# Attention backward on one core: row sums, transposes and casts of a softmax block moved by one to six units, and another order of the score products

## The chip, the cores and the metric

The kernel runs on one core of a Trainium2 chip. A core has a matrix engine (TensorE, PE in the profile, which keeps the loading of weights apart as PEld), three elementwise engines (VectorE or DVE, ScalarE or ACT, GpSimd or POOL), an engine that here only issues transfers (SyncE or SP), and 16 DMA engines. Each engine takes its own list of instructions in order and waits for the others through semaphores. The metric is the time of one execution on the device, in microseconds.

## The reference

Two attention blocks with 16 heads of width 28 over 2048 tokens of width 448 are evaluated forwards, their outputs are put side by side, and all gradients are returned (eight of them, and the output). Block A is linear attention. Block B, which fills most of the time, is softmax attention where all heads share one K and one V:

```python
q = (x @ wq).reshape(B, S, H, Dh)...        # 16 heads
k = x @ wk;  v = x @ wv                     # one for all heads
scores = einsum("bhqd,bkd->bhqk", q, k) * (Dh ** -0.5)
p = _softmax(scores, axis=-1)
o = einsum("bhqk,bkd->bhqd", p, v)
out = o... @ wo
...
_out, _vjp = jax.vjp(_f, A_x, ..., B_wo);  _grads = _vjp(grad_out)
```

Backwards, with do the gradient at o, the softmax needs dP = do v^T, dS = P * (dP - D) with D the row sums of do * o, then dQ = dS k, dK = dS^T q and dV = P^T do.

## The kernel before

Block A comes first, then the projections of block B, then the core of block B (the loop over `u`, L917), then the last products and gradients. The change touches only the core.

**Blocks and units.** The core works on 64 blocks `b`: 256 queries of two heads each. A block is cut into eight units of 256 keys, so there are 512 units, and unit `u` holds the scores of block u // 8. In unit `u` the scores S of that unit are made, together with dP (called D in the code, not to be mixed up with the row sums) of unit `w = u - 16`, two blocks earlier. Scores and dP are kept transposed: keys on the partitions, 512 columns for two times 128 keys, 256 queries each; one array for head 0 and one for head 1. Below, "position" is u mod 8, and S0, S1, D0, D1 are S and dP of heads 0 and 1. Each is two matmuls of 32 rows x 256 columns into one PSUM bank.

**What one unit does on each engine, in order.** The loop's body is the order, written out by hand (`tc.manual_schedule()`).

- TensorE: S and D (`rows_SD`, L663); in even units the products for o and dQ (`o_dq`) and dV (`dv_mm`), in odd units dK (`dk_m`, 16 matmuls at a time). Small products of other steps come in between: transposes of o (`onat_T`), transposes of do' (`don_T`), a part of an output projection.
- ScalarE: exp of S0 (L939), a copy `cp` of D1 (L953), exp of S1 (L997).
- VectorE: dsT of head 0, that is D0 times exp (L951), then the small steps that are due, then a 32x32 stream transpose `dsx` of a dsT made two units earlier (L1030).
- GpSimd: dsT of head 1, that is `cp` times exp (L956), and small steps, casts and copies.
- SyncE: every fourth unit a DMA transpose of the exponentials for dV (L999), in half of the blocks one of q for dK (L847), and five times in all one of o for the output projection (L988).

**Banks.** S has three PSUM banks in rotation: two are written in a unit and the third, `spare`, takes the small products (L921). After the units at positions 0, 2, 4 and 6 the spare bank is the one that S1 of the next unit writes; after positions 1, 3, 5 and 7 it is the one that S0 of the next unit writes. D has two banks, both written in each unit: D0's is free when VectorE's multiplication has read it, D1's when ScalarE's `cp` has.

**Steps that come once in a block.** `due(u, lag)` gives block `b` in unit 8b + lag. In order:

- lag 11 (position 3): o is scaled from its accumulator into `oTs` (VectorE, L972). The same accumulator holds dQ of block b - 2 in its other half, and a GpSimd cast (L978) stores that half as bf16 over q.
- lag 12 (position 4): `onat_T` transposes o into natural layout in the spare bank; `o_norm` takes the reciprocal of the softmax sums and makes `o_s` on VectorE, then on GpSimd `prod` = do * o (L812) and do' = `don` = do / sum (L815). The softmax sums are folded into do, and D into a column of do'.
- lag 13 (position 5): `row_D` sums `prod` over each head's columns (VectorE, L823), and GpSimd multiplies the result into the first column of `don` (L824).
- lag 14 (position 6): `don_T` transposes do' (L832, four matmuls into the spare bank); `don_copy` copies it as `doT` (VectorE, L839); `o_keep` casts `o_s` over do (GpSimd, L819), and for five blocks SyncE starts a DMA transpose of that.
- lag 16 (position 0 of the next block): the D products of block b begin, and read `doT`. The output projection's parts and their stores (L734) stand at position 0 too.

**The order of S and D.** `rows_SD` has a list `todo` of pairs (0 for S or 1 for D, head); each pair's first mention is its first 256 columns, its second mention the others. S of a head and D of a head lie in four different groups of 32 rows of the array.

Of the kernel before, what the change touches and what calls it, by code (L numbers as in the profile page):

```python
# [25 lines left out]
def kernel(  # L26
# [21 lines left out]
    nc = tc.nc  # L48
# [578 lines left out]
    NB = 64  # L627
    NU = NB * 8
    qT_B = [R1[:, g, :] for g in range(4)]
    vaug, kn, do_nat = vaug_, kn_, R2x[:, 0:NS, :]  # L630
    with ExitStack() as cs_:
# [17 lines left out]
        def eT(u):  # L649
            return ETs[u // 4 % 5][:, u % 4, :, :]  # L650
# [4 lines left out]
        def mmt(out, lhsT, rhs, pos, start, stop):  # L655
            nc.tensor.matmul(out, lhsT=lhsT, rhs=rhs, start=start, stop=stop, tile_position=pos,  # L656
                             skip_group_check=True)

        def blk(b):
            qc, pair = divmod(b, 8)  # L660
            return qc, pair, pair // 2, pair % 2

        def rows_SD(u, sp, dp):  # L663
            b, tp = divmod(u, 8)
            w = u - 16
            qc, pair, g, hp = blk(b)
            todo = [(0, 0), (0, 1), (1, 0), (1, 1)] * 2
            if sp is not None and dp is not None:
                todo = [(0, 0), (1, 0)] * 2 + [(0, 1), (1, 1)] * 2 if u % 2 else \
                    [(0, 0), (0, 1), (1, 0)] * 2 + [(1, 1)] * 2  # L670
            seen = {}
            for d in todo:
                if (dp if d[0] else sp) is None:
                    continue
                k, h = d
                t2 = seen.get(d, 0)
                seen[d] = 1
                t = 2 * tp + t2
                tc_ = slice(t * P, (t + 1) * P)
                oc = slice(t2 * 256, (t2 + 1) * 256)  # L680
                r = 64 * (1 - hp if k else hp) + 32 * h
                if k:
                    mmt(dp[h][:, oc], vT_rep[r:r + 32, tc_], doT[w // 8][r:r + 32, :], (r, 0), True, True)
                else:
                    mmt(sp[h][:, oc], kT_rep[r:r + 32, tc_], qT_B[g][r:r + 32, qc * 256:(qc + 1) * 256],
                        (r, 0), True, True)
# [7 lines left out]
        oTs = pp_.tile([P, 256], F32, name="oTs", bufs=1)  # L694
# [95 lines left out]
        def due(u, lag):  # L790
            b, r = divmod(u - lag, 8)
            return b if r == 0 and 0 <= b < NB else None

        def onat_T(b, bank):
            onp = bank[:, 0:P].rearrange("p (q h c) -> p q h c", q=2, h=2)
            r = 64 * (1 - b % 2)
            for qb in range(2):
                nc.tensor.transpose(onp[:, qb, :, :].rearrange("p h c -> p (h c)"), oTs[r:r + 64, qb * P:(qb + 1) * P],
                                    identF[r:r + 64, :], tile_position=(r, 0))
            onps[b] = onp  # L800

        def o_norm(b):
            onp = onps.pop(b)
            qc, pair, g, hp = blk(b)
            r_ = pw_.tile([P, 2, 2, 1], F32, name="rl")
            os_ = o_s[:]
            nc.vector.reciprocal(out=r_[:], in_=onp[:, :, :, 0:1])
            nc.vector.tensor_tensor(out=os_, in0=onp[:, :, :, :], in1=r_[:].to_broadcast([P, 2, 2, 32]), op=ALU.mult)  # L808
            rl[b] = r_
            dnv = do_nat[:, 2 * qc:2 * qc + 2, pair * 64:pair * 64 + 64].rearrange("p q (h c) -> p q h c", c=32)  # L810
            prod[b] = pw_.tile([P, 2, 2, 32], F32, name="prod", bufs=1)
            nc.gpsimd.tensor_tensor(out=prod[b][:], in0=dnv, in1=os_, op=ALU.mult)  # L812
            dn = pw_.tile([P, 2, 2, 32], BF16, name="don", bufs=2)
            don[b] = dn
            nc.gpsimd.tensor_tensor(out=dn[:], in0=dnv, in1=r_[:].to_broadcast([P, 2, 2, 32]), op=ALU.mult)  # L815
            o_nat[b] = dnv, os_

        def o_keep(b):
            nc.gpsimd.tensor_copy(out=o_nat[b][0], in_=o_nat.pop(b)[1])  # L819

        def row_D(b):
            Dq = pw_.tile([P, 2, 2, 1], F32, name="Dq")
            nc.vector.tensor_reduce(out=Dq[:, :, :, 0], in_=prod[b][:], axis=AX.X, op=ALU.add)  # L823
            nc.gpsimd.tensor_tensor(out=don[b][:, :, :, 0:1], in0=Dq[:], in1=rl[b][:], op=ALU.mult)  # L824

        def don_T(b, bank):
            r = 64 * (1 - b % 2)
            tp2 = bank[:, 0:P].bitcast(BF16)
            for qb in range(2):
                for h in range(2):  # L830
                    q = r + 32 * h
                    nc.tensor.transpose(tp2[q:q + 32, qb * P:(qb + 1) * P], don[b][:, qb, h, :], identB[:, :],  # L832
                                        tile_position=(0, q))
            tps2[b] = tp2

        def don_copy(b):
            r = 64 * (1 - b % 2)
            doT[b] = pw_.tile([P, 256], BF16, name="doT", bufs=2)
            nc.vector.tensor_copy(out=doT[b][r:r + 64, :], in_=tps2.pop(b)[r:r + 64, 0:256])  # L839
# [68 lines left out]
        with tc.manual_schedule():  # L908
# [8 lines left out]
            for u in range(NU + 28):  # L917
                w = u - 16
                hasS = u < NU
                hasD = 0 <= w < NU  # L920
                b0, b1, spare = ((SB[i] for i in ((0, 1, 2), (0, 2, 1), (1, 0, 2), (1, 2, 0))[u % 4]) if hasS else SB)  # L921
                sp = [b0, b1] if hasS else None
                dp = DB if hasD else None
                rows_SD(u, sp, dp)
                if u % 2 == 0:
                    o_dq((u - 4,), (u - 20,))
                if (b := due(u, 12)) is not None:
                    onat_T(b, spare)
                if (b := due(u, 14)) is not None:
                    don_T(b, spare)  # L930
                if op := out_part(u):
                    out_proj(*op, spare)
# [14 lines left out]
                if hasD:  # L947
                    dst = pd_.tile([P, 2, 512], BF16, name="dsT")
                    dsT[w] = dst
                    ew = eT(w)  # L950
                    nc.vector.tensor_tensor(out=dst[:, 0, :], in0=dp[0][:, :], in1=ew[:, 0, :], op=ALU.mult)  # L951
                    cp = pc_.tile([P, 512], BF16, name="cp")
                    nc.scalar.activation(out=cp[:, :], in_=dp[1][:, :], func=ACT.Copy)  # L953
                    if (b := due(u, 13)) is not None:
                        row_D(b)
                    nc.gpsimd.tensor_tensor(out=dst[:, 1, :], in0=cp[:, :], in1=ew[:, 1, :], op=ALU.mult)  # L956
                if (b := due(u, 13)) is not None and not hasD:
                    row_D(b)
                gq, iq = divmod(u % 64 - 30, 8)
                qq = u // 64 + 1  # L960
# [7 lines left out]
                if u % 8 == 3 and 0 <= (b := (u - 11) // 8) < NB + 2:  # L968
                    r = 64 * (1 - b % 2)
                    rr = slice(r, r + 64) if b < 2 else slice(0, P)  # L970
                    if b < NB:
                        nc.vector.tensor_scalar(out=oTs[rr, :], in0=oq[rr, 0:256], scalar1=fac[rr, b % 2:b % 2 + 1],  # L972
                                                scalar2=None, op0=ALU.mult)
                    if b >= 2:
                        qc, pair, g, hp = blk(b - 2)
                        rq = slice(64 * hp, 64 * hp + 64)
                        if b < NB:
                            nc.gpsimd.tensor_copy(out=qT_B[g][rq, qc * 256:(qc + 1) * 256], in_=oTs[rq, :])  # L978
                        else:
                            nc.vector.tensor_scalar(out=qT_B[g][rq, qc * 256:(qc + 1) * 256], in0=oq[rq, 0:256],  # L980
                                                    scalar1=scale, scalar2=None, op0=ALU.mult)
                if (b := due(u, 12)) is not None:
                    o_norm(b)
                if (b := due(u, 14)) is not None:
                    o_keep(b)
                    if b in (15, 31, 47, 55, 63):
                        t0, t1 = 2 * (b // 8) - 2 * (b < 48), 2 * (b // 8) + 2
                        nc.sync.dma_start_transpose(oTq[:, 4 * (t0 % 4):4 * (t0 % 4) + 4 * (t1 - t0), :],  # L988
                                                    do_nat[:, t0:t1, :].rearrange("p q c -> p (q c)"))
                if (b := due(u, 14)) is not None:  # L990
                    don_copy(b)
                if op:
                    out_store(*op, spare)
# [10 lines left out]
                if u % 2:  # L1004
                    b, i = divmod(u - 27, 8)
# [20 lines left out]
                if 0 <= y < NU:  # L1026
                    b, tp = divmod(y, 8)
                    if tp == 0:
                        dsx[b] = px_.tile([P, 8, 2, 2, 256], BF16, name="dsx")
                    nc.vector.transpose(  # L1030
                        out=dsx[b][:, tp, :, :, :].rearrange("p h t c -> p (h t c)").bitcast(F32),
                        in_=dsT[y][:, :, :].rearrange("p h c -> p (h c)").bitcast(F32))
# [113 lines left out]
```

## Time and profile before

The median of three runs is 1082.68 us (1082.59 to 1083.07).

| | us |
|---|---|
| profiled execution | 1082.19 |
| its span | 1080.1 |
| TensorE busy | 1050.2 |
| VectorE busy | 881.6 |
| ScalarE busy | 879.2 |
| GpSimd busy | 800.9 |
| TensorE's clock | full in all of the 40 slices |

The core runs from about 213 us, where the first exp starts, to about 1030 us. Of 300 to 998 us, 698 us, the engines are busy for 685.9 (TensorE), 683.6 (ScalarE), 653.0 (VectorE) and 635.7 (GpSimd). An entry of the timeline is: start, duration, engine, line, operation, output <- inputs, shapes, how many, and in brackets the idle time before it and who ended it. A line of the waits is: who waited, at which line, for whom: total, times, longest. Matmuls in the timeline overlap: several in different row or column groups of the array run at once. PSUM tiles go by the name of their pool: `aacc` is a bank of S (or the spare one), `agen` one of D, o, dQ or dK.

### The profile page before, as it was taken

The page shows a single profiled execution, that of the slowest core. Times are in us where ns is not written, and L with a number is a line of the kernel's source. Part 1 is how long each engine was busy: PE and PEld are TensorE (multiplying, and loading weights), DVE is VectorE, ACT ScalarE, POOL GpSimd, SP SyncE. Part 2 cuts the span into 40 slices and gives each one's busy share as a digit, 9 for nine tenths or more (in the row PEclk, how much of TensorE's full clock was granted, in tenths as well). Part 3 has the DMA queues.
Part 4 walks back from the last instruction along what each step waited for, and adds up shares of the span by engine and source line. Part 5 has one row for each costly group of instructions (what it writes and reads, how often), then busy time and mean ns, then how long its engine had stood idle before and what let it go on. Part 6 is the DMA issues. An engine that isn't in the chain of part 4 may idle for free.

```text
span 1080.1 us, 39972 instructions
## 1 busy us (share of the span) xinstructions
PE 1050.2 (97%) x16232; PEld 467.8 (43%) x16241; DVE 881.6 (82%) x1735; ACT 879.2 (81%) x1741; POOL 800.9 (74%) x1098
## 2 busy tenths in 40 slices
PE   9999999989999999999999999999999999999998
PEld 4555545433444444444444444444444444444434
DVE  7887400559999999999999999999999999999943
ACT  6463122589999999999999999999999999999622
POOL 6001252228998998899889989988998899888881
PEclk9999999999999999999999999999999999999999
DMA  9759898079999999999999999999999999999973
GB/s 269 157 109 195 178 203 230 13 142 195 197 193 191 175 191 186 190 190 202 176 183 186 193 197 184 194 191 175 194 189 188 191 196 194 178 180 177 213 149 92
DMA packets 689936, 195.14 MB, mean 181 GB/s; under 512 B 670616, under 2 KB 687792, under 8 KB 689752
## 3 DMA queue, kind: packets, MB, share of 16 engines
q1 hardware_dynamic: 680152, 179.92, 97.8%
q0 software_dynamic: 4640, 8.71, 2.6%
q10 hardware_dynamic: 4960, 3.96, 1.4%
q8 instruction: 127, 2.08, 0.8%
q14 instruction: 57, 0.47, 0.1%
HBM read 12.60 MB, written 10.84 MB: 22 GB/s over the span
## 4 chain that ended last, share of the span: by engine, by line
PE 43%; POOL 27%; ACT 15%; issue 8%; DVE 7%; POOLq 0%; ACTq 0%; DVEq 0%
POOL dsT L956 20%; PE agen L81 14%; PE agen L656 13%; ACT cp L953 8%; PE aacc L656 7%; PE aacc L81 7%; ACT eT L997 5%; DVE dsx L1030 3%; ACT eT L939 2%; POOL prod L812 2%; POOL R L978 1%; DVE dsT L951 1%; POOL don L815 1%; POOL qst L843 1%; PE aacc L832 1%
## 5 line engine op out<-in xcount | busy, mean ns | idle before, releaser
L956 POOL TENSOR_TENSOR dsT<-cp,eT 128x512 bf16<-128x512 bf16 x512 | 587.8, 1157 | 69.9 <-ACT cp L953 62.1
L1030 DVE STREAM_TRANSPOSE dsx<-dsT 128x512 f32<-128x512 f32 x512 | 357.5, 698 | 2.1 <-POOL dsT L956 0.9
L951 DVE TENSOR_TENSOR dsT<-agen,eT 128x512 bf16<-128x512 f32 x512 | 341.0, 666 | 20.7 <-PE agen L656 17.1
L656 PEld LDWEIGHTS <-R 128*32 128x32 bf16 (+1 forms) x9104 | 212.2, 93 | 313.2 <-issue 270.4
L939 ACT ACTIVATE eT<-aacc 128x512 bf16<-128x512 f32 x512 | 320.4, 626 | 20.8 <-PE aacc L656 17.3
L953 ACT ACTIVATE cp<-agen 128x512 bf16<-128x512 f32 x512 | 320.9, 627 | 12.9 <-PE agen L656 11.9
L997 ACT ACTIVATE eT<-aacc 128x512 bf16<-128x512 f32 x512 | 326.6, 638 | 0.0
L656 PE MATMUL agen<-doT,R 32*128 32x256 bf16 x2048 | 279.9, 269 | 2.9 <-DVE dsT L951 2.1
L656 PE MATMUL aacc<-R,R 32*128 32x256 bf16 (+1 forms) x2240 | 268.7, 268 | 3.6 <-ACT eT L939 1.8
L656 PE MATMUL agen<-dsx,qX 32*32 32x512 bf16 x4096 | 267.6, 375 | 0.0
L656 PE MATMUL agen<-dsT,R 128*32 128x256 bf16 x2048 | 188.4, 276 | 0.5 <-issue 0.5
L656 PE MATMUL agen<-eT,R 128*32 128x256 bf16 x2048 | 188.3, 276 | 0.1
L656 PEld LDWEIGHTS <-qX 32*32 32x32 bf16 x4096 | 79.8, 89 | 114.7 <-issue 54.3
L656 PE MATMUL aacc<-eN,don 128*32 128x512 bf16 x1024 | 96.7, 379 | 0.0
L81 PEld LDWEIGHTS <-R 128*128 128x128 bf16 (+1 forms) x517 | 40.7, 98 | 43.2 <-issue 11.0
L406 POOL COPY pk<-R 128x256 bf16<-128x256 bf16 x4 | 1.6, 397 | 73.8 <-DVE R L366 73.7
L81 PE MATMUL agen<-R,R 128*128 128x448 bf16 (+1 forms) x174 | 41.1, 360 | 1.3 <-issue 0.6
L823 DVE TENSOR_REDUCE Dq<-prod 128x4 f32<-128x128 f32 x64 | 18.3, 286 | 26.1 <-POOL prod L812 26.1
L812 POOL TENSOR_TENSOR prod<-R,o_s 128x128 f32<-128x128 bf16 x64 | 27.6, 432 | 11.2 <-DVE o_s L808 11.2
L843 POOL COPY qst<-R 128x512 bf16<-128x512 bf16 x56 | 34.3, 613 | 1.3 <-DMA qX<-qst 1.3
L656 PEld LDWEIGHTS <-don 128*32 128x32 bf16 x1024 | 33.8, 97 | 1.2 <-issue 0.7
L422 DVE TENSOR_TENSOR osb<-aacc,pr 64x448 bf16<-64x448 f32 x2 | 1.2, 617 | 38.8 <-DMA out_dram<-osb 24.2
(233 smaller groups left out, 975.7 us busy)
## 6 DMA issues: line engine op xcount, KB each, us to landing
out_dram<-osb ACTq DMA_DIRECT2D x22, 112.0 KB
eN<-eT SPq DMA_TRANSPOSE x128
xa<-in_A_x_dram SPq DMA_DIRECT2D x8, 224.0 KB
ga<-in_grad_out_dram SPq DMA_DIRECT2D x4, 448.0 KB
xa<-in_grad_out_dram POOLq DMA_DIRECT2D x4, 448.0 KB, 5.8
out_dram<-wdq POOLq DMA_DIRECT2D x8, 224.0 KB, 4.1
eT<-in_grad_out_dram SPq DMA_DIRECT2D x4, 448.0 KB
eT<-in_B_x_dram SPq DMA_DIRECT2D x4, 448.0 KB
```

The lines of the kernel that those rows point to most:

```text
L81: nc.tensor.matmul(out_ap, lhsT=lhsT, rhs=rhs, start=start, stop=stop, tile_position=(0, 0))
L656: nc.tensor.matmul(out, lhsT=lhsT, rhs=rhs, start=start, stop=stop, tile_position=pos, skip_group_check=True)
L812: nc.gpsimd.tensor_tensor(out=prod[b][:], in0=dnv, in1=os_, op=ALU.mult)
L815: nc.gpsimd.tensor_tensor(out=dn[:], in0=dnv, in1=r_[:].to_broadcast([P, 2, 2, 32]), op=ALU.mult)
L823: nc.vector.tensor_reduce(out=Dq[:, :, :, 0], in_=prod[b][:], axis=AX.X, op=ALU.add)
L843: eng.tensor_copy(out=st.rearrange("p (b s) a j -> p b s a j", s=2)[:, :, s, :, :], in_=src.unsqueeze(2).to_broadcast([P, 4, 4, 32]))
L939: nc.scalar.activation(out=eT(u)[:, 0, :], in_=sp[0][:, :], func=ACT.Exp, scale=scale)
L951: nc.vector.tensor_tensor(out=dst[:, 0, :], in0=dp[0][:, :], in1=ew[:, 0, :], op=ALU.mult)
L953: nc.scalar.activation(out=cp[:, :], in_=dp[1][:, :], func=ACT.Copy)
L956: nc.gpsimd.tensor_tensor(out=dst[:, 1, :], in0=cp[:, :], in1=ew[:, 1, :], op=ALU.mult)
L997: nc.scalar.activation(out=eT(u)[:, 1, :], in_=sp[1][:, :], func=ACT.Exp, scale=scale)
L1030: nc.vector.transpose(out=dsx[b][:, tp, :, :, :].rearrange("p h t c -> p (h t c)").bitcast(F32), in_=dsT[y][:, :, :].rearrange("p h c -> p ...
```

## The change

Five edits, all in the core's loop.

1. `row_D` at lag 14 instead of 13 (position 6).
2. `don_T` and `don_copy` at lag 15 instead of 14 (position 7, an odd unit; `don_T` stands behind S and D and ahead of dK).
3. The cast of dQ's half of `oTs` on GpSimd at lag 17 (position 1 of the next block) instead of lag 11 (position 3); the last two blocks keep their cast on VectorE at position 3.
4. `o_keep`, and with it the five DMA transposes of o, at lag 16 instead of 14 (position 0 of the next block).
5. In units that have both S and D, the odd ones issue S0, D0, D1, S1 and then the same four again, where they issued S0, D0 twice and then S1, D1 twice. Even units keep S0, S1, D0 twice and then D1 twice.

```diff
             todo = [(0, 0), (0, 1), (1, 0), (1, 1)] * 2
             if sp is not None and dp is not None:
-                todo = [(0, 0), (1, 0)] * 2 + [(0, 1), (1, 1)] * 2 if u % 2 else \
-                    [(0, 0), (0, 1), (1, 0)] * 2 + [(1, 1)] * 2
+                todo = [(0, 0), (1, 0), (1, 1), (0, 1)] * 2 if u % 2 else [(0, 0), (0, 1), (1, 0)] * 2 + [(1, 1)] * 2
...
-                if (b := due(u, 14)) is not None:
+                if (b := due(u, 15)) is not None:
                     don_T(b, spare)
...
-                    if (b := due(u, 13)) is not None:
+                    if (b := due(u, 14)) is not None:
                         row_D(b)
                     nc.gpsimd.tensor_tensor(out=dst[:, 1, :], in0=cp[:, :], in1=ew[:, 1, :], op=ALU.mult)
-                if (b := due(u, 13)) is not None and not hasD:
+                if (b := due(u, 14)) is not None and not hasD:
                     row_D(b)
...
                     if b >= 2:
                         qc, pair, g, hp = blk(b - 2)
                         rq = slice(64 * hp, 64 * hp + 64)
-                        if b < NB:
-                            nc.gpsimd.tensor_copy(out=qT_B[g][rq, qc * 256:(qc + 1) * 256], in_=oTs[rq, :])
-                        else:
+                        if b >= NB:
                             nc.vector.tensor_scalar(out=qT_B[g][rq, qc * 256:(qc + 1) * 256], in0=oq[rq, 0:256],
                                                     scalar1=scale, scalar2=None, op0=ALU.mult)
+                if (b := due(u, 17)) is not None and b >= 2:
+                    qc, pair, g, hp = blk(b - 2)
+                    rq = slice(64 * hp, 64 * hp + 64)
+                    nc.gpsimd.tensor_copy(out=qT_B[g][rq, qc * 256:(qc + 1) * 256], in_=oTs[rq, :])
                 if (b := due(u, 12)) is not None:
                     o_norm(b)
-                if (b := due(u, 14)) is not None:
+                if (b := due(u, 16)) is not None:
                     o_keep(b)
...
-                if (b := due(u, 14)) is not None:
+                if (b := due(u, 15)) is not None:
                     don_copy(b)
```

## The prediction

> **What bounds the kernel now.** I read the page first, then the waits of the long middle stretch (300 to 998 us), then the timeline of one block of eight units, instruction by instruction.
>
> ```profile
> PE 1050.2 (97%) x16232; PEld 467.8 (43%) x16241; DVE 881.6 (82%) x1735; ACT 879.2 (81%) x1741; POOL 800.9 (74%) x1098
> ```
>
> All four compute engines are nearly full, and TensorE's 97% counts a matmul as busy while it merely stands in the pipeline, so shares settle nothing. The waits of 300 to 998 us do:
>
> ```profile
> POOL dsT L956 <- ACT cp L953: 50.6, 144, 0.9
> PEld L832 <- POOL don L824: 26.7, 56, 0.9
> DVE Dq L823 <- POOL prod L812: 23.1, 55, 0.6
> ...
> ACT eT L939 <- PE aacc L656: 11.6, 54, 0.3
> ```
>
> 56 blocks lie there. In nearly every one TensorE waits for the last column of do' (L824; 0.48 us each), and VectorE for the product whose rows it sums (0.42). One block, positions 2 to 7, then 0 and 1 (u mod 8), starts at 698.94 and ends at 711.21:
>
> ```profile
> 699.88 0.67 ACT L953 ACTIVATE cp<-agen 128x512 bf16<-128x512 f32 x1
> ...
> 700.42 0.28 PE L656 MATMUL aacc<-R,R 32*128 32x256 bf16 x1
> ...
> 700.54 0.32 PE L656 MATMUL agen<-doT,R 32*128 32x256 bf16 x2
> 700.61 0.28 PE L656 MATMUL aacc<-R,R 32*128 32x256 bf16 x1
> 700.71 0.27 PE L656 MATMUL agen<-doT,R 32*128 32x256 bf16 x1
> 700.85 0.69 ACT L939 ACTIVATE eT<-aacc 128x512 bf16<-128x512 f32 x1
> ...
> 700.91 1.04 PE L656 MATMUL agen<-dsx,qX 32*32 32x512 bf16 x16
> ...
> 703.57 1.15 POOL L956 TENSOR_TENSOR dsT<-cp,eT 128x512 bf16<-128x512 bf16 x1
> ...
> 704.68 0.43 POOL L812 TENSOR_TENSOR prod<-R,o_s 128x128 f32<-128x128 bf16 x1
> ...
> 705.15 0.29 DVE L823 TENSOR_REDUCE Dq<-prod 128x4 f32<-128x128 f32 x1 [0.30 <-POOL prod L812]
> ...
> 705.58 0.22 POOL L824 TENSOR_TENSOR don<-Dq,rl 128x4 bf16<-128x4 f32 x1
> ...
> 705.85 0.23 PE L832 MATMUL aacc<-identB,don 128*32 128x128 bf16 x2
> ...
> 705.98 0.65 DVE L951 TENSOR_TENSOR dsT<-agen,eT 128x512 bf16<-128x512 f32 x1
> ...
> 706.50 0.28 PE L656 MATMUL aacc<-R,R 32*128 32x256 bf16 x1
> 706.66 0.29 DVE L839 COPY doT<-aacc 64x256 bf16<-64x256 bf16 x1
> 706.68 0.26 PE L656 MATMUL agen<-doT,R 32*128 32x256 bf16 x1
> ...
> 707.01 0.26 PE L656 MATMUL aacc<-R,R 32*128 32x256 bf16 x1
> ...
> 707.33 1.05 PE L656 MATMUL agen<-dsx,qX 32*32 32x512 bf16 x16
> ```
>
> Three things to see. First, the chain at position 6: product on POOL (704.68), row sum (705.15), column (705.58), transposes (705.85). VectorE's multiplication slips with it to 705.98, so position 7's first D product waits until that is done (706.68), and its S1 until the doT copy has emptied the spare bank (707.01). Second, 700.54: two D products in 0.32 us, the second starting 0.05 after cp ended (699.88 + 0.67 = 700.55). It sits in D's second bank; that release holds up the end of S/D in every odd unit. Third, ScalarE's three operations per unit start 0.48 apart when nothing holds them: 1.43 a unit, 11.5 a block, its floor.
>
> TensorE's S/D start times (698.94, 700.42, 701.88, 703.52, 705.01, 706.50, 708.31, 709.56, 711.21) give unit lengths of 1.48, 1.46, 1.64, 1.49, 1.49, 1.81, 1.25, 1.65: 12.27 us.
>
> **The change part by part.** I carry this block forward by hand, zero at 698.94, with spacings read from it. Release to dependent instruction: 0.05. Last needed S start to exp: 0.31. S/D end to the next kind of product: 0.20 after its last start. dK to the next unit's S/D: 0.98. A freed ScalarE operation lasts 0.60.
>
> (1) Row sum one unit later (13 to 14). VectorE's 0.42 wait goes. In position 5 it now goes straight from multiplication to stream transpose, and position 6's multiplication starts at 6.5 instead of 7.04. The product has long been ready then. POOL's column operation (0.22) now stands behind position 5's dsT multiplication as well: dsT of position 4 at 4.6, spacing 1.12, product 0.38, don 0.37, dsT of position 5 1.13, so the column runs 7.60 to 7.82. VectorE's sum ends at 7.4, so POOL's queue sets it.
>
> (2) Transposes from position 6 to 7 (14 to 15). Position 6 loses the wait and four transposes. S/D of 6 starts at 6.07; D1 waits for cp (6.16) until 6.22, its second half at 6.33; products at 6.52; four rounds and dV take 0.77 as at position 4; position 7 starts at 7.29 (now 7.56): 0.27 earlier. There the transposes stand alone between 32-row S/D and dK. The rows: 0.20 into the other shape, 0.06 for the second pair, 0.16 out (o to S/D takes 0.21 with a 0.11 product, so 0.10 beyond the product, plus 0.055): 0.42, against 0.20 for S/D to dK directly. So 0.22 of added TensorE time. The column at 7.82 plus 0.05 is before the 7.96 at which transposes could start: no wait, with 0.1 to spare.
>
> The Trainium skill speaks against this part: TensorEngine Tiling (Array Packing), Key Properties, says that changing the tiling mode drains the TensorE. The trace agrees in direction (0.20 instead of 0.11 between starts); a full drain would be the 0.27 that one S product lasts, on two switches instead of 0.20 and 0.16, and by that the block would lose 0.07 + 0.11 = 0.18 and the whole gain 62 x 0.18 = 11 us of what is worked out below. I go by the rows.
>
> (3) doT's copy now follows in position 7, and the unit right behind it uses it, and its bank for S0. VectorE: multiplication at 8.0, copy behind it 8.6 to 8.9, S0 possible from 8.95. TensorE arrives at 9.16. Hidden behind dK, slack 0.2; if VectorE ran later than that, every microsecond would be paid.
>
> (4) Odd order S0, D0, D1, S1 twice. The products take four row groups either way; the quoted 700.61 line follows D1 there, not S0's round. What changes: D1's wait for cp now stands ahead of the second halves of S0 and D0. TensorE's end of S/D does not move (D1, plus 0.11), but exp and VectorE's multiplication start from D1's release plus 0.31. In position 3: D1 at 1.66, exp at 1.98 instead of 1.91. At 5 S1 (waiting for o_s) does the same: 5.08 instead of 5.01. Cost 0.07 to 0.09 per odd unit on ScalarE's chain. In the walk below it mostly disappears, because S/D of the next unit starts when dK ends and not when exp does; and a late start shortens cp from 0.68 to 0.60. I take nothing at 3 and 5, and let 7 and 1 come out of the walk.
>
> (5) dQ cast (0.39) from position 3 to 1 of the next block, o's cast (0.29) from 6 to 0. POOL's sum stays: 8 x 1.13 + 0.37 + 0.38 + 0.37 + 0.2 + 0.25 = 10.6, with two qst copies 11.7, in a 12.0 block. Both leave the stretch from 3 to 6 where the column is made and enter 0 and 1, where dsT waits for cp. The oTs rewrite (2.6) follows the cast (1.3 to 1.65) by a unit. Cost zero, cover: two units before VectorE needs dsT. Without the cover: 0.68. The five DMA transposes of o on SP move two units, behind position 7's eN transpose (5.4 us on SP): issue, wait and 2.9 us make 8.3 of the eight units (12 us) before their reader. Hidden; five late ones would cost a few us in all. SP itself: two eN transposes (10.9) and one qX (1.3) make 12.2 in half of the blocks and 10.9 in the others: its mean, 11.6, stays under 12.0.
>
> **The sum.** Positions 2 to 5: 6.07 as now. Position 6: exp 6.52, cp 7.00 to 7.60. Position 7: start 7.29, D1 at 7.65, second halves 7.65, last product 7.76, transposes 7.96 and 8.02, dK 8.18, end 9.16; exp 7.97, cp 8.45 to 9.05. Position 0: D1 is free, so S/D takes 0.38 and not 0.50; with 0.75 behind it as now, it ends at 10.29; exp 9.59, cp 10.07 to 10.67. Position 1: D1 waits for that cp until 10.72, last product 10.83, dK 11.03, end 12.01. So 12.01 against 12.27, 0.26 less. Position 7 gets longer (1.87), position 1 too (1.72): the wait for cp takes over what don_T's wait gave up. exp spacings give 12.35 as mean block from unit 26 to 506. About 62 blocks x 0.26 = 16 us. The profiled execution took 1082.19 (span 1080.1), 0.5 below the median: 1066 either way.
>
> **Rivals.**
> A. Slower: the new order of odd units. If ScalarE, not TensorE, paces positions 1, 3, 5 and 7, the later exp of (4) is paid four times on top of the walk: 0.07 to 0.09 each, 0.28 to 0.36 a block against the 0.26 gained. It decides from 0.065 an odd unit on; at 0.09 the block is 0.10 longer than now: 1084 to 1089. For it: ScalarE's starts stand 0.48 apart from position 2 to 4. Against it: over the whole block ScalarE has 12.27 - 11.5 = 0.8 us to spare.
> B. Nothing: only exp at position 7 counts, 8.06 now and 7.97 then, and the rest is lost to D1's waits: 0.03 or less a block, 1081 to 1083. For it: position 6's gain of 0.27 shrinks to 0.09 there. Against: dK's end moves by 0.21.
> C. Larger: VectorE's freed 0.42 and POOL's earlier dsT also shorten positions 3 to 5 and 1, down to 11.75: 1050. ScalarE's floor, 11.5, would be 1034; nothing in the trace reaches it for a whole block.
> D. Less: POOL late. With qst copies and the store's DMA (0.58) in one block the column slips 0.26, past the 0.1 to spare. If the transposes wait 0.15 in every block: 12.16, 1075.
>
> **How the numbers follow.** Forecast (about 1058 to 1072) 0.44, C 0.12, D 0.16, B 0.06, A 0.22. About 0.2% is what a measurement here can tell from no change. Faster: 0.44 + 0.12 + 0.16 = 0.72; same 0.06; slower 0.22. The range reaches from C's near half (1052) to most of A (1087); the forecast's own is 1058 to 1072.
>
> **What would show it.** L832's wait for L824 and L823's for L812 gone; block near 12.0; position 6 near 1.22, positions 7 and 1 near 1.87 and 1.72; exp of odd units later by some 0.08 against their S/D start. It is wrong if L832 still waits for L824 (POOL), if S0 of position 0 waits for L839 (VectorE), or if ScalarE's odd units lengthen without TensorE waiting.

## The result: 0.55% faster, a third of what was forecast

The changed kernel takes 1077.26 us (median of four runs, 1076.81 to 1078.0) against 1082.88 before: ratio 0.9945, 95% interval 0.9928 to 0.9962. It is faster, clear of noise, but by 5.6 us and not by 16, and 1077 lies outside the forecast's own range (1058 to 1072). The profiled execution took 1077.67 us (span 1075.9).

The waits of 300 to 998 us in the changed kernel (who waited, for whom: total us, times, longest) (line numbers differ by one or less from those of before, save dQ's cast, which has its own place now):

```profile
POOL dsT L955 <- ACT cp L952: 44.2, 114, 0.6
DVE dsT L950 <- PE agen L656: 21.3, 85, 0.3
PEld L831 <- POOL don L823: 12.1, 57, 0.3
PEld aacc L797 <- ACT eT L998: 12.1, 57, 0.2
ACT eT L938 <- PE agen L656: 12.0, 58, 0.4
```

VectorE's wait for the product is gone (23.1 us), as forecast. The row of don_T and POOL's column is not: 12.1 us are left of 26.7, in all 57 blocks. It counts the idle time ahead of don_T's weight load (PEld), and not that ahead of its products (PE). The timeline of one block shows what each of them waited for (positions 6 and 7; S/D of position 6 starts at 702.90):

```profile
704.34 0.65 ACT L998 ACTIVATE eT<-aacc 128x512 bf16<-128x512 f32 x1
704.46 0.21 POOL L823 TENSOR_TENSOR don<-Dq,rl 128x4 bf16<-128x4 f32 x1
704.55 0.28 PE L656 MATMUL aacc<-R,R 32*128 32x256 bf16 x2
...
704.67 0.27 PE L656 MATMUL aacc<-R,R 32*128 32x256 bf16 x1
704.87 0.28 PEld L831 LDWEIGHTS <-don 128*32 128x32 bf16 x4 [0.21 <-POOL don L823]
704.88 0.60 ACT L938 ACTIVATE eT<-aacc 128x512 bf16<-128x512 f32 x1
...
705.04 0.29 PE L831 MATMUL aacc<-identB,don 128*32 128x128 bf16 x4
705.26 1.04 PE L656 MATMUL agen<-dsx,qX 32*32 32x512 bf16 x16
```

The column is ready at 704.46 + 0.21 = 704.67. The last S/D product starts at 704.67, so by my spacing of 0.20 the transposes were possible at 704.87, and that is when their weights are loaded. The products start at 705.04, which is 0.05 after the second exp of position 6 has ended (704.34 + 0.65 = 704.99). That exp empties the bank that S1 had in position 6, and that bank is the spare one of position 7. In blocks 4 to 59 the transposes start 0.050 to 0.052 after that exp, without exception, and 0.11 to 0.42 after the column. The sum of waits does not show this wait at all. Its 12.1 us are 0.21 a block, the step from the last S/D product to the weight load (0.20 in the median block), and in 54 of 56 blocks not a wait for POOL; the run with a bank of its own, below, still has the row (12.8 us, 57 times, of 300 to 990 us, where the changed kernel has 12.1). The chain of waits shows it:

```profile
630.53 0.63 ACT cp L952
631.16 0.50 ACT eT L998
631.66 0.04 issue
631.70 0.29 PE aacc L831 x4
631.99 0.97 PE agen L656 x16
```

The chain now runs through the exp into the transposes and on into dK. POOL, 27% of the chain before, has 1% of it.

Unit lengths from S/D start to S/D start (positions 2 to 7, 0, 1; the measured ones are medians over the middle of the core):

| | 2 | 3 | 4 | 5 | 6 | 7 | 0 | 1 | sum |
|---|---|---|---|---|---|---|---|---|---|
| before, the block shown | 1.48 | 1.46 | 1.64 | 1.49 | 1.49 | 1.81 | 1.25 | 1.65 | 12.27 |
| forecast | 1.48 | 1.46 | 1.64 | 1.49 | 1.22 | 1.87 | 1.13 | 1.72 | 12.01 |
| measured | 1.46 | 1.48 | 1.62 | 1.47 | 1.25 | 2.09 | 1.09 | 1.77 | 12.22 |

Seven positions are within 0.05. Position 7 is 0.22 longer than forecast, and that is the whole difference from the walked 12.01.

Below, "mean block" is the time from exp of unit 26 to exp of unit 506 over 60: 12.347 before (255.18 to 996.03), 12.277 after (255.34 to 991.98). Sixty times 0.070 is 4.2 of the 4.5 us between the two profiled executions. "Median block" is the median of blocks 4 to 59, from position 2 to position 2: 12.29 before, 12.22 after; the walk's and the expectations' block lengths are to be held against it. In part of the runs the granted clock is 0.998 instead of 1.0, and in profiled executions of that kind exp of unit 26 comes 1 to 2 us later (256.8 to 257.3 against 254.9 to 255.8 us), so small differences are read from the blocks and not from the whole time.

### The profile page after: what moved, and what is told of

Read it like the earlier page. It is cut to its first block, busy times and chain, and to the rows that moved or that the text cites. A ratio compares the mean times of both kernels' runs of the same rounds, so it can differ in the third digit from the quotient of the medians.

```text
span 1075.9 us, 39956 instructions
## 1 busy us (share of the span) xinstructions
PE 1040.5 (97%) x16232; PEld 471.5 (44%) x16241; DVE 887.8 (83%) x1735; ACT 873.2 (81%) x1741; POOL 799.8 (74%) x1098
## 4 chain that ended last, share of the span: by engine, by line
PE 69%; ACT 18%; issue 8%; DVE 3%; DMA 1%; POOL 1%; ACTq 0%; DVEq 0%; POOLq 0%
PE agen L656 30%; PE agen L81 14%; PE aacc L656 14%; ACT cp L952 10%; PE aacc L81 7%; ACT eT L998 6%; PE aacc L831 2%; PE aacc L797 1%; ACT eT L938 1%; DVE dsx L1031 1%; DVE dsT L950 1%; DMA dsx<-R 1%; PE aacc L85 0%; DMA qX<-qst 0%; POOL dsT L955 0%
## 5 line engine op out<-in xcount | busy, mean ns | idle before, releaser
L950 DVE TENSOR_TENSOR dsT<-agen,eT 128x512 bf16<-128x512 f32 x512 | 348.0, 680 | 35.9 <-PE agen L656 26.4
L656 PEld LDWEIGHTS <-R 128*32 128x32 bf16 (+1 forms) x9104 | 204.3, 94 | 323.5 <-issue 293.0
L938 ACT ACTIVATE eT<-aacc 128x512 bf16<-128x512 f32 x512 | 310.4, 606 | 22.8 <-PE agen L656 15.2
L952 ACT ACTIVATE cp<-agen 128x512 bf16<-128x512 f32 x512 | 311.8, 609 | 12.7 <-PE agen L656 10.9
L998 ACT ACTIVATE eT<-aacc 128x512 bf16<-128x512 f32 x512 | 318.1, 621 | 0.0
L656 PE MATMUL aacc<-R,R 32*128 32x256 bf16 (+1 forms) x2240 | 261.5, 269 | 3.7 <-ACT eT L938 1.8
L656 PE MATMUL agen<-eT,R 128*32 128x256 bf16 x2048 | 177.8, 276 | 0.7 <-DVE oTs L971 0.6
L656 PE MATMUL agen<-dsT,R 128*32 128x256 bf16 x2048 | 177.8, 276 | 0.0
L656 PE MATMUL aacc<-eN,don 128*32 128x512 bf16 x1024 | 91.4, 379 | 0.0
L971 DVE TENSOR_SCALAR oTs<-agen,fac 128x256 f32<-128x256 f32 (+1 forms) x64 | 30.3, 474 | 0.8 <-POOL R L982 0.5
L516 ACT ACTIVATE wdq<-agen 128x448 bf16<-128x448 f32 x16 | 8.7, 543 | 24.7 <-PE agen L81 24.7
```

The lines of the kernel that those rows point to most:

```text
L938: nc.scalar.activation(out=eT(u)[:, 0, :], in_=sp[0][:, :], func=ACT.Exp, scale=scale)
L998: nc.scalar.activation(out=eT(u)[:, 1, :], in_=sp[1][:, :], func=ACT.Exp, scale=scale)
```

## The experiments

Theory 1: don_T at position 7 waits for the exp that empties its bank. Theory 2: it waits for POOL's column, as the sum of waits seems to say. Theory 3: leaving the 32-row shape for a transpose takes 0.36 us.

**A bank of its own.** The bank `oq` accumulates o and dQ in its first 256 columns, and the others are free.

```diff
-            tp2 = bank[:, 0:P].bitcast(BF16)
+            tp2 = oq[:, 256:384].bitcast(BF16)
```

> The changed kernel, but don_T writes its 256 bf16 columns into the free second half of the bank that accumulates o and dQ, instead of the spare S bank. Theory 1 (bank): in the changed kernel don_T at position 7 starts 0.05 us after the second exp of position 6 has emptied that bank, 0.36 us after the last S/D product, and not 0.20 as I had it. With a bank of its own it starts 0.20 after S/D: 0.16 to 0.17 earlier, dK and everything behind it too, block 12.05 instead of 12.22, 62 x 0.17 = 10 us: about 1067. Theory 2 (column): the profile names POOL's column L823 as what don_T waits for; then nothing changes: 1077. Theory 3 (shape): leaving the 32-row shape for a transpose simply takes 0.36; nothing changes: 1077.

1069.57 us, ratio 0.9879 (0.9864 to 0.9894), mean block 12.145, median 12.06. In this kernel one of the gradients, out_5, which comes from dQ, is wrong (by 0.54, relative), because the transposes wipe what dQ had accumulated in the same bank; a later run with another way of turning keeps it. The same number and kind of instructions run, so the time can be compared. Position 7 of one block:

```profile
700.72 0.65 ACT L998 ACTIVATE eT<-aacc 128x512 bf16<-128x512 f32 x1
700.83 0.22 POOL L823 TENSOR_TENSOR don<-Dq,rl 128x4 bf16<-128x4 f32 x1
...
701.05 0.27 PE L656 MATMUL aacc<-R,R 32*128 32x256 bf16 x1
701.25 0.29 PE L831 MATMUL agen<-identB,don 128*32 128x128 bf16 x4
...
701.47 1.05 PE L656 MATMUL agen<-dsx,qX 32*32 32x512 bf16 x16
```

The transposes start at 701.25, while that exp still runs (until 701.37): 0.20 after the last S/D product. Position 7 takes 1.92 instead of 2.09 and the seven others are as they were. Theory 1 holds; 2 and 3 fall. It is 7 to 8 us of the missing 10.

**The column earlier.** Row sums back at lag 13, everything else as changed.

```diff
-                    if (b := due(u, 14)) is not None:
+                    if (b := due(u, 13)) is not None:
                         row_D(b)
...
-                if (b := due(u, 14)) is not None and not hasD:
+                if (b := due(u, 13)) is not None and not hasD:
                     row_D(b)
```

> The changed kernel with the row sum back at lag 13, a unit further ahead of don_T. Theory 1 (bank): don_T still starts 0.05 after exp of position 6, so no gain; VectorE waits for the product again (0.3 to 0.4 at position 5) and its multiplication at position 6 comes 0.4 later, which holds D0 of position 7: block 12.25 to 12.35, 1079 to 1085. Theory 2 (column): the column is ready a unit earlier, don_T's wait goes, block 12.05: 1067 to 1070 (less by what VectorE loses).

1079.98 us, 0.9972 (0.9963 to 0.9982), mean block 12.286, median 12.22. The column now ends 1.3 us before the transposes and they start no sooner: in 50 of 56 blocks 0.05 after the exp. The sum of waits of this run shows what moving the row sum had taken away, VectorE's wait for the product and behind it TensorE's for VectorE's multiplication:

```profile
DVE Dq L822 <- POOL prod L811: 17.9, 56, 0.6
...
PE agen L656 <- DVE dsT L950: 10.5, 56, 0.4
```

These waits cost little here. The blocks are 0.009 longer than in the changed kernel, 0.5 us over sixty; the rest of the 0.27% between the two ratios lies outside them. The transposes wait for the exp in either case.

**The old order in odd units.** The changed kernel with S0, D0 twice and then S1, D1 twice.

```diff
-                todo = [(0, 0), (1, 0), (1, 1), (0, 1)] * 2 if u % 2 else [(0, 0), (0, 1), (1, 0)] * 2 + [(1, 1)] * 2
+                todo = [(0, 0), (1, 0)] * 2 + [(0, 1), (1, 1)] * 2 if u % 2 else \
+                    [(0, 0), (0, 1), (1, 0)] * 2 + [(1, 1)] * 2
```

> The changed kernel with the old order of S and D in odd units (S0, D0 twice, S1, D1 twice). My step (4): TensorE's end of S/D does not depend on it, exp of odd units starts 0.07 to 0.09 earlier with the old order, and that is mostly hidden: block 12.20 to 12.23, 1075 to 1077. Rival A of the prediction (ScalarE pays the new order): block up to 0.2 shorter, 1065 to 1070. Opposite rival (four row groups abreast save TensorE 0.1 to 0.2 in each odd unit): block 0.3 longer, 1090 or more.

1073.69 us, 0.992 (0.9906 to 0.9933), mean block 12.188: 0.09 shorter. The median block is 12.15, 0.07 shorter, where I had allowed 0.02 at most. The new order is a loss. Position 5 in the changed kernel and in this run:

```profile
701.43 0.28 PE L656 MATMUL aacc<-R,R 32*128 32x256 bf16 x1
701.43 0.28 PE L656 MATMUL agen<-doT,R 32*128 32x256 bf16 x2
...
701.62 0.28 PE L656 MATMUL aacc<-R,R 32*128 32x256 bf16 x2
...
701.94 0.60 ACT L938 ACTIVATE eT<-aacc 128x512 bf16<-128x512 f32 x1
```

```profile
700.18 0.28 PE L656 MATMUL aacc<-R,R 32*128 32x256 bf16 x1
...
700.30 0.27 PE L656 MATMUL aacc<-R,R 32*128 32x256 bf16 x1
...
700.61 0.60 ACT L939 ACTIVATE eT<-aacc 128x512 bf16<-128x512 f32 x1
```

With the new order S0's second half waits until 701.62, where S1's bank comes free, and exp starts 0.51 after the unit did. With the old order the half starts at 700.30 and exp 0.43 after. Most of the 0.08 runs down ScalarE's chain. In medians from the start of position 2, the copy at position 5 ends at 6.09 instead of 6.15, S/D of position 7 starts at 7.21 instead of 7.28, and the second exp of position 6, on which the transposes hang through the bank, ends at 8.06 instead of 8.11.

**The casts back.** The changed kernel with dQ's cast at position 3 and o's at position 6, as before the change.

```diff
-                        if b >= NB:
+                        if b < NB:
+                            nc.gpsimd.tensor_copy(out=qT_B[g][rq, qc * 256:(qc + 1) * 256], in_=oTs[rq, :])
+                        else:
                             nc.vector.tensor_scalar(out=qT_B[g][rq, qc * 256:(qc + 1) * 256], in0=oq[rq, 0:256],
...
-                if (b := due(u, 17)) is not None and b >= 2:
-                    qc, pair, g, hp = blk(b - 2)
-                    rq = slice(64 * hp, 64 * hp + 64)
-                    nc.gpsimd.tensor_copy(out=qT_B[g][rq, qc * 256:(qc + 1) * 256], in_=oTs[rq, :])
...
-                if (b := due(u, 16)) is not None:
+                if (b := due(u, 14)) is not None:
                     o_keep(b)
```

> The changed kernel with the casts of dQ and of o back at lag 11 (position 3) and 14 (position 6). By my POOL walk dsT of position 4 then starts up to 0.37 later, and with it product, do' and column: the column ends at 8.0 to 8.2 of the block where don_T starts at 8.17 for its bank, so don_T is 0.0 to 0.1 later: 1077 to 1083. If POOL's place of the casts is what the measured gain comes from, the block returns to 12.28: 1082.

1076.88 us, 0.9949 (0.9936 to 0.9961), mean block 12.274, median 12.22: nothing. The column ends 0.15 before the transposes (median) instead of 0.36, still soon enough.

**Parts alone, on the kernel before.**

```diff
-                todo = [(0, 0), (1, 0)] * 2 + [(0, 1), (1, 1)] * 2 if u % 2 else \
-                    [(0, 0), (0, 1), (1, 0)] * 2 + [(1, 1)] * 2
+                todo = [(0, 0), (1, 0), (1, 1), (0, 1)] * 2 if u % 2 else [(0, 0), (0, 1), (1, 0)] * 2 + [(1, 1)] * 2
```

> The kernel before with the new order of S and D in odd units and nothing else. Taking the new order out of the changed kernel brought 0.07 us a block, since exp of odd units starts 0.07 to 0.09 later under it. Theory 1: that delay is paid here too, because dsT of position 4, product and column hang on ScalarE's copy of position 4: block 12.30 to 12.40, 1084 to 1090. Theory 2: the order only costs where don_T waits for an exp's bank, so here nothing: 1083. Theory 3 (four row groups abreast shorten S/D): 1070 to 1078.

1084.99 us, 1.0022 (1.0012 to 1.0033), mean block 12.391, 0.04 longer (median 12.37, 0.08 longer): the time is at the low end of theory 1, and against theories 2 and 3.

The other part alone is don_T and the copy of doT at lag 15:

```diff
-                if (b := due(u, 14)) is not None:
+                if (b := due(u, 15)) is not None:
                     don_T(b, spare)
...
-                if (b := due(u, 14)) is not None:
+                if (b := due(u, 15)) is not None:
                     don_copy(b)
```

> The kernel before with don_T and the copy of doT at lag 15 and nothing else (row sums at 13, casts and order as before). If the parts add: the changed kernel less the row sums' 0.27% and plus the order's 0.25%, so about 0.9947 of before: 1077 to 1079. don_T starts 0.05 after exp of position 6 or 0.20 after S/D, whichever is later, never 0.05 after the column. If instead row sum and transposes only work together, 1081 to 1083.

1079.33 us, 0.9976 (0.9967 to 0.9986), mean block 12.299, median 12.28. The gain is between the two expectations: less than the sum of the parts asked for (0.9947), but not nothing. In all 56 blocks the transposes start 0.05 after the exp or 0.20 after S/D, whichever is later. With the row sum still at position 5, VectorE's wait makes its multiplication of position 6 late, and D0 of position 7 waits for that:

```profile
706.02 0.29 DVE L823 TENSOR_REDUCE Dq<-prod 128x4 f32<-128x128 f32 x1 [0.31 <-POOL prod L812]
...
706.85 0.65 DVE L951 TENSOR_TENSOR dsT<-agen,eT 128x512 bf16<-128x512 f32 x1
...
707.55 0.27 PE L656 MATMUL agen<-doT,R 32*128 32x256 bf16 x1 [0.26 <-DVE dsT L951]
...
707.92 0.29 PE L832 MATMUL aacc<-identB,don 128*32 128x128 bf16 x4
```

The block is 0.11 longer than in the run with the old order above (12.188), which has the row sum and the casts moved as well. If the casts are worth nothing there, as they were with the new order, the row sum's move is worth some 0.11 a block with the old order, and with the new one, as shown, 0.01.

**Own bank, all gradients kept.** The turning is a matmul with the identity that is not marked as the start of an accumulation (`start` is False). In the same rows of the bank dQ's own first product, at position 4, is marked so.

```diff
-            tp2 = bank[:, 0:P].bitcast(BF16)
+            tp2 = oq[:, 256:512]
...
-                    nc.tensor.transpose(tp2[q:q + 32, qb * P:(qb + 1) * P], don[b][:, qb, h, :], identB[:, :],
-                                        tile_position=(0, q))
+                    mmt(tp2[q:q + 32, qb * P:(qb + 1) * P], don[b][:, qb, h, :], identB[:, :], (0, q), False, True)
```

> The changed kernel with do' turned by a matmul with the identity into the free half of the accumulators' bank, without clearing that bank's flags, and read back as fp32. In the run with a bank of its own the transposes cleared what dQ had accumulated in the same bank, so dQ and out_5 there are not the reference's; here they are. Bank theory: as there, don_T 0.20 after S/D, block 12.06 to 12.10 (the copy reads fp32, 0.42 instead of 0.29 us, of which up to 0.04 may show): 1068 to 1072.

1071.72 us, 0.9905 (0.9885 to 0.9925), mean block 12.177, median 12.17, with out_5 right. The copy from fp32 takes 0.42 instead of 0.28 (medians), and 0.03 of the mean block shows; the median block is longer than I expected (12.06 to 12.10), and the time lies within what I expected.

The same with the old order of odd units (the two diffs, this one and the old order's, together):

> The same with the old order of S and D in odd units. ScalarE's copy of position 6 comes 0.08 earlier in the run with the old order, and D1 of position 7 and what follows hang on it: block 11.97 to 12.02, 1063 to 1067. If the old order had only helped by freeing the spare bank earlier, nothing is left to gain: as the run before it, 1068 to 1072.

1065.21 us, 0.9843 (0.9827 to 0.986), mean block 12.069, median 12.05. Faster than both kernels: 1.6% below the one before. The order is worth 0.11 a block here, more than with the shared bank (0.09), so its cost was not only that the bank came free later.

On this version two more runs. First, D1 ahead of S1, but both behind the halves of S0 and D0:

```diff
-                todo = [(0, 0), (1, 0)] * 2 + [(0, 1), (1, 1)] * 2 if u % 2 else \
+                todo = [(0, 0), (1, 0)] * 2 + [(1, 1), (0, 1)] * 2 if u % 2 else \
```

> The fastest version so far (do' into the accumulators' bank, old order), with D1 ahead of S1 in odd units but both still behind the second halves of S0 and D0. Theory (wait ahead of the halves): the new order costs because D1's wait for ScalarE's copy stands ahead of S0's second half and so delays exp; here it does not, so nothing changes: ratio to before 0.984 to 0.985, 1064 to 1066 where before takes 1082. Rival (it is D1 before S1 that costs, whatever stands behind): as the run with the new order, 0.990, 1071.

1065.46 us, 0.9846 (0.9831 to 0.986), mean block 12.065, median 12.01: no change. What the new order loses is lost because waiting products stand ahead of the second halves of S0 and D0.

Second, the casts back once more, by the same diff as above:

> The fastest version so far with the two casts back at positions 3 and 6. Where don_T waited for its bank they were worth nothing. Here the column ends 0.06 to 0.26 before don_T, and with dQ's cast back at position 3 it ends up to 0.3 later. Theory (cover): now the casts' place matters, don_T waits for the column in many blocks: ratio 0.987 to 0.994, 1068 to 1075. Rival (POOL has room either way): 0.984 to 0.985, 1064 to 1066.

1069.59 us, 0.989 (0.9873 to 0.9906), mean block 12.128, median 12.07. The casts' place, worth nothing above, is worth 0.06 a block here. POOL's order in one block of this run:

```profile
695.86 0.39 POOL L977 CAST R<-oTs 64x256 bf16<-64x256 f32 x1
...
696.23 1.16 POOL L955 TENSOR_TENSOR dsT<-cp,eT 128x512 bf16<-128x512 bf16 x1
697.34 0.44 POOL L812 TENSOR_TENSOR prod<-R,o_s 128x128 f32<-128x128 bf16 x1
697.72 0.41 POOL L815 TENSOR_TENSOR don<-R,rl 128x128 bf16<-128x128 bf16 x1
698.08 1.17 POOL L955 TENSOR_TENSOR dsT<-cp,eT 128x512 bf16<-128x512 bf16 x1
...
699.20 0.23 POOL L824 TENSOR_TENSOR don<-Dq,rl 128x4 bf16<-128x4 f32 x1
...
699.53 0.29 PE L656 MATMUL agen<-identB,don 128*32 128x128 bf16 x4
```

With dQ's cast ahead the column ends at 699.43. Here the product comes 0.20 behind the last S/D product (699.34) and is not held yet. In the block before, it is:

```profile
687.20 0.27 PE L656 MATMUL agen<-doT,R 32*128 32x256 bf16 x1
687.28 0.23 POOL L824 TENSOR_TENSOR don<-Dq,rl 128x4 bf16<-128x4 f32 x1
...
687.56 0.29 PE L656 MATMUL agen<-identB,don 128*32 128x128 bf16 x4
```

The column ends at 687.51, and the product starts 0.05 behind it, 0.36 behind the last S/D product. In 35 of 56 blocks it starts less than 0.06 behind the column; with the casts moved it is 8.

## Why the prediction failed, by its own steps

- **Step (2), the transposes at position 7: the step that failed.** Its account of TensorE time was right: in the run with its own bank it is 0.20 into the transposes and 0.22 from the first of them to dK, as taken from the rows (0.06 and 0.16), and position 6 came out at 1.25 for 1.22. But "at which transposes could start" looked at the end of S/D and at the column, and not at the bank. The bank table stood in the code: the spare bank of position 7 is S1's bank of position 6. At position 6 the same rule held and cost nothing, because S/D and two rounds of products lay ahead of the transposes: in the kernel before they start 0.32 or more after the exp that frees their bank. Moved to stand right behind S/D, they met it: they start at 8.17 after the block's start, where the walk has 7.96. The walk held what was needed to see it: copy of position 6 from 7.00, exp 0.48 behind it, its end 0.60 to 0.65 later, at about 8.1. The wait is 0.17 in the block shown and 0.13 in the mean, 8 us. The sign that I had set for it, a wait of L832 for L824, could not tell: that row stands in the sum of waits with the bank's wait and without it.
- **Step (4), the order of odd units: right in mechanism, wrong in size.** Exp is 0.08 late, as worked out for positions 3 and 5. "I take nothing at 3 and 5" was wrong: I never walked the block with the old order, and so took as given what the order costs in the walk itself. It is 0.04 a block on the kernel before, 0.09 on the changed one, 0.11 without the bank's wait. Rival A had the direction right, the later exp is paid, at 0.01 to 0.03 an odd unit and not the 0.065 from which it decides.
- **Step (1), the row sums: right.** VectorE's wait is gone, the column ends where forecast (7.80 for 7.82 after the block's start). Undoing it costs 0.27% by the whole times, but only 0.01 a block. I had not said that this step and step (2) need each other: with the old order the transposes' move alone is worth 0.05 a block, and 0.16 with the row sum's and the casts'.
- **Step (3), doT's copy: right.** It ends at 705.92, and S/D of position 0 starts at 706.23.
- **Step (5), the casts: right at zero as the kernel stands**, and covered: the bank's wait leaves the column 0.36 us to spare, and casts at their old place take 0.21 of it. In the version with neither the bank's wait nor the new order their place is worth 0.5%. With the old order alone the column still has 0.30 to spare, so by these margins it is the bank's wait that covers them; no run puts the casts back with the old order alone.
- **The walk** gave 12.01 for the block; without the bank's wait 12.06 was measured. The other positions held. About the forecast gain is reached only in another kernel, with neither the bank's wait nor the new order: a mean block 0.28 shorter than before, 17 us over sixty.
- **Rival D** had the right place (transposes that wait about 0.15 a block, 1075) under the wrong cause: not POOL.

The Trainium skill's rule that a change of the tiling mode drains the TensorE (TensorEngine Tiling (Array Packing), Key Properties) did not decide it. The 0.36 us in the changed kernel look like it, but with another bank the same change of shape takes 0.20, less than the 0.27 that one S product lasts in this profile, where the ends of matmuls are modelled.

## What to carry to other kernels

When a step is moved to another place in a hand-written order, list again everything its first instruction needs at the new place: inputs, but also who last used its output buffer and when that reader is done; at the old place the answer may have been hidden. Walk the old and the new version by the same rules, also for an edit that looks like tidying; and put an operation that waits behind those that don't, since those behind it were held up with it here. A part that measures as nothing may be covered by a wait that another part leaves in: test it again when that wait is gone. And look in a sum of waits at which instruction waited: a weight load's idle time is not that of its product.

## What the runs showed of the hardware that was not expected

TensorE does not start all matmuls in the order of the list: in the block of before shown above, with the order S0, S1, D0, S0, S1, D0, D1, D1, these are the copy of position 5 and S/D of position 6:

```profile
704.44 0.59 ACT L953 ACTIVATE cp<-agen 128x512 bf16<-128x512 f32 x1
...
705.01 0.28 PE L656 MATMUL aacc<-R,R 32*128 32x256 bf16 x2
705.02 0.33 PE L656 MATMUL agen<-doT,R 32*128 32x256 bf16 x2
...
705.13 0.27 PE L656 MATMUL aacc<-R,R 32*128 32x256 bf16 x2
```

Two D products in 0.33 us, the second starting at 705.08, 0.05 after ScalarE's copy of position 5 has ended: that can only be D1, as the second halves of S0, S1 and D0 all start 0.12 after the first, at 705.13. It starts 0.05 ahead of the second halves of S0 and S1, which stand before it in the list and wait for their own rows. PSUM — Partial Sum Buffer, Engine vs sequencer instructions, in the Trainium skill says that matmuls start and complete in program order; for different groups of rows this trace differs. A matmul that waits for a semaphore, on the other hand, does hold up those behind it whose rows and banks are free: above, S0's second half stands behind S1 and starts with it at 701.62, and not 0.12 after its first half, at 701.55.
